# One-core causal attention with a hard-swish layer pair: finer first-layer operations, scores up to four units ahead, three TensorE modes, new keys

## The chip, the cores and the metric

The kernel runs on one core of a Trainium2 chip. The metric is device time in microseconds (us) of one execution, as the median of several. The engines are TensorE (PE: matmuls, and PEld: its weight loads), VectorE (DVE), ScalarE (ACT), GpSimd (POOL) and SyncE (SP, which issues most of the transfers).

## What is computed

The reference is causal attention followed by two dense layers with a hard-swish between them:

```python
scores = (q @ k^T) / 8;  scores[j > i] = -1e9        # 4 batches, 12 heads, 448 positions, 64 wide
attn = softmax(scores);  x = (attn @ v)              # x as 1792 tokens x 768
h = x @ w_in                                         # 768 x 2048
g = h * clip(h + 3, 0, 6) / 6
out = g @ w_out                                      # 2048 x 768
```

Inputs and output are float32; the weights arrive as 64-bit words, from which the kernel makes float32 itself.

## The kernel before

**Units.** Attention is cut into 24 units: a unit is one batch and one pair of heads (`unit`, line 420). A unit loads Q, K and V; multiplies Q and K into scores (line 490, rows in four tiles of 112); reduces each row's bound with VectorE (line 505); takes exponentials with ScalarE, which also sums them (line 512); inverts the sums (lines 522 and 523) and scales the rows (`scaled`, lines 531 and 533); transposes 112x112 blocks on PE (line 553), moves them out of the accumulator memory PSUM, and multiplies them with V (line 566). Its result is one 128-row chunk of x for its batch, split into a high and a low part (`x_split`). Scores use 64 rows of the array for each of the two heads at once, products with V use 64 columns for each head, all else uses the whole array. Units 0 to 5 make their scores from the raw float32; later ones split Q and K first and use three terms.

**Layers.** A product of split operands takes three matmuls (`triple`, lines 640 to 642): high by high, high by low, low by high. Four batches of 448 tokens (g = 0 to 3) go through. `first_layer(g)` for the first two batches makes 16 chunks of the hidden layer, each summed over six chunks of x; each chunk of weights needs words turned into floats by VectorE (lines 603, 605 and 608), a high part from ScalarE (line 361) and a low part (line 373). Batch 0's second layer follows in part in `early_products`; the rest of the work runs through sums and differences of half matrices (`middle`, `last_first`, `last_second`), which the change touches through keys alone.

**What sets the order.** Nothing is issued at run time by choice. `Flow` (line 111) is a planner: every piece of work is an operation with a key, an engine or a choice of engines, a duration and dependencies. `Flow.run` plays the program through and at each moment gives a free engine the ready operation with the lowest key whose buffers are free; the order so found is the order of instructions. PE operations have a mode: `tiled` is true for scores and products with V, false for the rest. The planner counts `SWITCH / 2` for each change and stays in a mode while an operation of that mode has a key no more than `KEEP` above the lowest (lines 229 to 233). A unit's key is its `step` plus `UNIT[at]`; loads come at that key plus `T_LOAD + LOADS[at]`, V's another `T_V` later, scores at `K_SCORES`, transposes at `K_TURN`, the product with V at `K_PRODUCT` after it. Units of batch 0 have the lowest keys.

**Limits.** A unit's scores wait for the product of the unit two earlier, or `DEPTH` earlier in batch 0 (line 498). There are eight PSUM banks; a unit's scores take six (`ps`), the first-layer accumulators at most `MOST["mo"]`. Before the order is played out, `Flow.WARM` small matmuls run (line 1092); between 20 and 36 us the planner may put small filler matmuls (line 1072) into gaps of PE.

Of the kernel before, what the change touches and what calls it, by code (L numbers as in the profile page):

```python
# [19 lines left out]
C = 112  # L20
# [8 lines left out]

T_FIRST = -113
T_PACE = 4
T_EARLY = 8
T_EACH = 11
T_LATE = 74
T_DENSE = 7.25
T_LOAD = -8
T_W = 10
T_WLOAD = 9  # L40
T_XA = 166
T_X = 175
T_LAST = 182
T_PAIR = 10.5
T_SECOND = T_LAST + 8 * T_PAIR
T_SECOND_GROUP = 72
T_MID = 120
T_BACK = 40
T_WORDS = 77
M_LOAD = 20  # L50
E_WORDS = 6.5
K_SCORES = 0
K_TURN = 6.5
K_TURNS = 0.6
K_PRODUCT = 14
K_GATE = 5
KEEP_FULL = 0
KEEP_TILED = 6.5
N_RAW = 6
DEPTH = 3  # L60
A_FIRST = 4
D_FIRST = 0.4
T_V = 11
FINE = 3
W_FROM = 3
W_BEHIND = 4
UNIT = [-80, -17, 5, 2.5, 0.5, -1, -2, -1.5, 5.5, 0.5, -6.5, -3, -3.5, -8, -2.5, -4.5, -1, -1.5, -6, -4.5, -2.5, 1, -4, 3]
LOADS = [-70, -38, -8, 10, 0, -10, 12, -14, -22, -4, -20, -14, 10, 4, -12, 2, -8, -12, -2, -28, -10, -4, 4, -6]
K_KEEP = -4
K_G = 4  # L70
GATE_FROM = 1
WORDS = [1, 8, -6, 4, -3, 7, -5, 0, -4, 3, -6, 0, 6, -2, 7, -4, 2, 4, 2, 3, -2, 2, -8, -4, 8, 3, -7, 5]
T_ISSUE = 0.36
NORM_LAG = 1.5
A_LAG = 0

BUFS = dict(
# [6 lines left out]
    qk="d qk", op="d op", wf="d wf", sf="d sf", x="d x", pt="d pt", pr3="d pr3", pr20="d pr20", xq="d xq", xc="d xc", gt="d gt", gm="d gm", so="d so",  # L84
    ps="b s most ps", tp="b s most", av="b s", mo="b mo", c="b c",
)
MOST = dict(qk=3, op=4, wf=4, sf=6, x=8, pt=6, pr3=4, pr20=5, xq=6, xc=21, gt=12, gm=9, so=3, s=8, most=8, ps=8, mo=2, c=8)

ORDERED = dict(sf=3, wd=0, wh=1, wl=2, xq=3, xc=3, gt=3, gm=3, pr3=4, pr2=5, pr1=6, pr20=9, pt=7, op=8)

# [20 lines left out]
class Flow:  # L111
# [3 lines left out]

    FILL, SPARE_TIME, FILL_FROM, FILL_UNTIL = 0.2, 0.25, 20.0, 36.0
    BEGIN, LATENCY = 0.8, 0.12
    SWITCH = 0.4
    TAIL = dict(PE=.1, D=.085, A=.105, P=.04, SP=0)

    KEEP = KEEP_FULL, KEEP_TILED
    QUEUE, WARM = 8, 4
    DMA_PACKET, DMA_RATE, DMA_LANES, DMA_LATENCY = 0.008, 23e3, 16, 2.1
    COLD = dict(PE=(4.5, 1.6), SP=(7.5, 1.3))
    FIRST_UNTIL, FIRST_DMA = 34.0, 1.18
# [4 lines left out]
        self.filler, self.idle, self.spare = None, 0.0, 1  # L130
        self.ops, self.wrote, self.readers, self.landed = [], {}, {}, []

    def op(self, key, ways, parts, r=(), tiled=False, nbytes=0):

        w = [x for _, _, ws in parts for x in ws]
        bufs = {x[0] for x in list(r) + w if isinstance(x[0], Buf)}
        o = Op((key, len(self.ops)), ways, parts, bufs, nbytes)
        o.tiled = tiled
        for b in bufs:
            b.refs += 1  # L140
        before = {}
        for x in list(r) + w:
            if x in self.wrote:
                a, i = self.wrote[x]
                before[a] = max(before.get(a, 0), i)
        for x in w:
            for a in self.readers.pop(x, ()):
                before[a] = len(a.parts) - 1
        for x in r:
            self.readers.setdefault(x, []).append(o)  # L150
        for i, (_, _, ws) in enumerate(parts):
            for x in ws:
                self.wrote[x] = o, i
        before.pop(o, None)
        for a, i in before.items():
            a.then.append((o, i))
        o.waits = len(before)
        self.ops.append(o)
        return o

    def run(self):

        events, out = [], []
        lists = {e: [] for e in ("PE", "D", "A", "P", "SP")}
        busy = dict.fromkeys(lists, self.BEGIN)
        self.dma, self.mode, self.port, tick = 0.0, False, 0.0, 0
        left = len(self.ops)

        def post(t, what, x):
            nonlocal tick  # L170
            tick += 1
            heappush(events, (t, tick, what, x))

        post(self.BEGIN, "idle", None)
        turns, seen = {k: [] for k in ORDERED.values()}, set()
        for o in self.ops:
            if not o.waits:
                post(0.0, "ready", o)
            for b in o.bufs - seen:
                if b.kind in ORDERED:  # L180
                    turns[ORDERED[b.kind]].append((o.key, o))
            seen |= o.bufs
        for x in turns.values():
            x.sort(key=lambda a: a[0], reverse=True)
        while events:
            now = events[0][0]
            while events and events[0][0] <= now + 1e-9:
                _, _, what, x = heappop(events)
                if what == "ready":
                    for e, (_, lag) in x.ways.items():  # L190
                        if lag:
                            post(now + lag, "way", (e, x))
                        else:
                            insort(lists[e], (x.key, x), key=lambda a: a[0])
                elif what == "way":
                    if x[1].ends is None:
                        insort(lists[x[0]], (x[1].key, x[1]), key=lambda a: a[0])
                elif what == "end":
                    left -= 1
                    for b in sorted(x.bufs, key=lambda b: b.at):  # L200
                        b.refs -= 1
                        if not b.refs:
                            self.slots[b.tag].append(b.slot)
                            for t in b.uses:
                                self.free[t] += 1
            for e, cand in lists.items():
                if busy[e] > now + 1e-9:
                    continue
                cand[:] = [a for a in cand if a[1].ends is None]
                chosen, limit = None, 1e9  # L210
                for _, o in cand:
                    if o.key[0] > limit:
                        break
                    if e in o.port and (self.port > now + 1e-9 or e == "D" and self.turn_of_pool(o, lists["P"], busy, now)):
                        continue
                    need = {}
                    for b in o.bufs:
                        if not b.held:
                            for t in b.uses:
                                need[t] = need.get(t, 0) + 1  # L220
                    for b in o.bufs:
                        if not b.held and b.kind in ORDERED:
                            x = turns[ORDERED[b.kind]]
                            while x and x[-1][1].ends is not None:
                                x.pop()
                            if x[-1][1] is not o:
                                need[b.tag] = len(self.ops)
                    if all(self.free[t] >= n for t, n in need.items()):
                        if e != "PE" or o.tiled == self.mode:
                            chosen = o, need  # L230
                            break
                        if not chosen:
                            chosen, limit = (o, need), o.key[0] + self.KEEP[self.mode]
                if e == "PE":
                    if not chosen:
                        self.spare = min(self.spare, self.free["b"])
                    else:
                        self.fill(now, out)
                if chosen:
                    self.start(chosen[0], e, now, chosen[1], out, busy, post)  # L240
        assert not left, [o.key for o in self.ops if o.ends is None][:5]
        out.sort(key=lambda a: a[:2])
        return out
# [21 lines left out]
    def start(self, o, e, now, need, out, busy, post):  # L265
# [3 lines left out]
            b.held, b.slot = True, self.slots[b.tag].popleft()  # L269
        t, o.ends = now, []  # L270
        if e == "PE" and o.tiled != self.mode:
            t += self.SWITCH / 2
            self.mode = o.tiled
        for d, emit, _ in o.parts:
            out.append((t, len(out), e, emit, o.port))
# [26 lines left out]
def tile_causal_attention_hardswish_moe(ctx: ExitStack, tc: tile.TileContext, q, k, v, w_in, w_out, out):  # L302
    nc = tc.nc
# [38 lines left out]
        if not port:  # L342
            o.port = set()

    def pe(key, parts, r, tiled=False):
        flow.op(key, {"PE": (1, 0)}, [(d, lambda e, g=g: g(), w) for d, g, w in parts], r, tiled)

    def dma(key, packet, o, i, r=(), w=(), queue="SP", rows=128):
# [71 lines left out]
    def unit(b, p):  # L420
        at = NPAIR * b + p
# [67 lines left out]
                    qx, kx = (ap(xs[x])[:, 0], ap(xs[y])[:, 1]) if xs else (qa(0), qa(1))  # L489
                    nc.tensor.matmul(score(e, i), qx[m, c], kx[m, :w], start=n == 0, stop=n == len(terms) - 1)  # L490

        cost, more = (1.667e-3, .06) if raw32 else (1.25e-3, .08)
        for a, two in enumerate(((1, 0), (3, 2)) if at == 0 else ((3, 2), (1, 0))):
            key = t + 2 * a + K_SCORES
            pe(
                key,
                [(cost * C * (i + 1) + more, lambda i=i: products(i), [(ps[e, i][0], i) for e in range(2)] + [("turn",)]) for i in two],
                (halves_[0] if at == a == 0 else reads) + [("unit", at - (2 if b else DEPTH))], True,
            )
            for i in two:  # L500
                w = C * (i + 1)
# [40 lines left out]
        for e in range(2):  # L542
            for js, ph in zip(GROUPS, pairs):
# [8 lines left out]
                    for n, (i, j) in enumerate(blocks):  # L552
                        nc.tensor.transpose(ap(tp)[:C, C * n:C * n + C], row_of(pr, e, i)[:, C * j:C * j + C], ident)  # L553

                pe(key, [(.096 * len(blocks) + .03, turn, [(tp, 0)])], [pk[e, i] for i in sorted({i for i, _ in blocks})])
                move(
                    key + .1, o, lambda ph=ph, e=e, o=o: ap(ph)[:, e, :o], lambda tp=tp, o=o: ap(tp)[:C, :o],
                    [(tp, 0)], [(ph, e)], {"A": 1, "D": (1, .4 if b else D_FIRST)},
# [9 lines left out]
                        start=(j == 0), stop=(j == NC_ - 1),  # L568
                    )

        pe(t + K_PRODUCT, [(10 * C * 1.667e-3, times_v, [(av, 0), (av, 1), ("unit", at)])], deps, True)
        if b < 2:
            x_split(t + 16, b, p, av, S)
        else:
# [71 lines left out]
    def first_layer(g):  # L646
# [5 lines left out]
        for i in range(NF):  # L652
            t = t0 + 3 * i
            wh, wl = weights(g, i, t)
            acc, r = bank("mo"), buf("r", [128, S])
            few = 1 if not g and i < FINE else 2
            for c0 in range(0, NK, few):
                cs = range(c0, c0 + few)

# [429 lines left out]
    b = Buf("b", [128, 512], F32)  # L1089
    b.slot = BANKS["b"] - 1  # L1090
    for _ in range(Flow.WARM):
        nc.tensor.matmul(ap(b)[:C, :C], warm, warm, start=True, stop=True)

    sync = mybir.DependencyInfo(mybir.DependencyClass.Sync, mybir.DependencyReason.DATA)
    older = None
# [46 lines left out]
```

## Time and profile before

| | us |
|---|---|
| median of 3 runs | 583.35 (583.2 to 584.42) |
| the profiled execution, its own time | 583.93 |
| its span, first to last instruction | 582.2 |
| PE busy | 573.8 |
| DVE busy | 486.7 |
| ACT busy | 405.7 |
| POOL busy | 233.4 |

The busy times are those of one profiled execution. PE's matmuls overlap one another and their ends are modelled, so its busy time is no measure of lost time; the starts of its instructions in the timeline are. "Idle before" in a row is the time in which an engine had nothing to do, with what ended it.

### The profile page before, as it was taken

To read this page: it belongs to the slowest core of one execution; us is meant where nothing else is said; L and a number is where in the kernel's file an instruction comes from. 1 tells how busy PE (TensorE), PEld (TensorE's weight loads), DVE (VectorE), ACT (ScalarE), POOL (GpSimd) and SP (SyncE) were. 2 spreads that over 40 slices of the span, in tenths; PEclk is the share of its full clock that TensorE was granted. 3 is DMA by queue.
4 is the path that set the end of the run, shared out by engine and by line. 5 is a ranking of instruction groups with operands and counts; after the bars stand their busy time and mean duration, and the time that the engine had idled before them with its cause. 6 is when DMAs were issued, how large, how long until landed. Compare 5 with 4: busy or idle time off the path is not lost.

```text
span 582.2 us, 10686 instructions
## 1 busy us (share of the span) xinstructions
PE 573.8 (99%) x3496; PEld 502.5 (86%) x3496; DVE 486.7 (84%) x1093; ACT 405.7 (70%) x973; POOL 233.4 (40%) x226
## 2 busy tenths in 40 slices
PE   8999999999999999999999999999999999999997
PEld 5667988988888788888988989899999999999996
DVE  5899999899689787999998668999888799985652
ACT  6997885888757666899988968576555586454530
POOL 2678889874447344776274212034000042100000
PEclk9999999999999999999999999999999999999999
DMA  8958999967579898999832254441211424443411
GB/s 235 334 184 278 315 319 362 395 230 233 179 267 303 258 385 267 329 381 304 301 114 76 94 165 145 160 128 56 82 55 55 128 64 135 133 133 111 138 64 48
DMA packets 61352, 115.59 MB, mean 199 GB/s; under 512 B 6512, under 2 KB 36592, under 8 KB 61296
## 3 DMA queue, kind: packets, MB, share of 16 engines
q1 hardware_dynamic: 60576, 114.34, 59.5%
q10 hardware_dynamic: 720, 0.57, 0.3%
q8 instruction: 27, 0.44, 0.3%
q14 instruction: 29, 0.24, 0.1%
HBM read 83.39 MB, written 31.49 MB: 197 GB/s over the span
## 4 chain that ended last, share of the span: by engine, by line
PE 88%; DMA 5%; DVE 3%; ACT 2%; issue 1%; SPq 0%; DVEq 0%; ACTq 0%
PE b L640 24%; PE b L641 23%; PE b L642 23%; PE b L566 7%; PE b L553 6%; PE b L490 5%; DMA gl<-in_v_dram 2%; DMA wd<-in_w_in_dram 1%; DMA wd<-in_w_out_dram 1%; ACT d L512 1%; DVE b L603 1%; DVE d L608 1%; DVE b L505 1%; DVE b L605 1%; ACT gl L512 0%
## 5 line engine op out<-in xcount | busy, mean ns | idle before, releaser
L640 PE MATMUL b<-d,wh 128*128 128x448 f32 x624 | 231.4, 371 | 0.7 <-ACT d L512 0.7
L641 PE MATMUL b<-d,wh 128*128 128x448 f32 x624 | 226.3, 363 | 0.0
L642 PE MATMUL b<-d,wl 128*128 128x448 f32 x624 | 225.7, 362 | 0.0
L640 PEld LDWEIGHTS b<-d,wh 128*128 128x128 f32 x624 | 117.2, 188 | 10.6 <-ACT d L512 1.2
L642 PEld LDWEIGHTS b<-d,wl 128*128 128x128 f32 x624 | 116.9, 187 | 9.0 <-POOL wl L373 0.4
L641 PEld LDWEIGHTS b<-d,wh 128*128 128x128 f32 x624 | 117.2, 188 | 6.3
L361 ACT CAST wh<-wd 128x768 fp32r<-128x768 f32 x88 | 73.6, 836 | 70.1 <-PE b L641 61.5
L373 DVE TENSOR_TENSOR wl<-wd,wh 128x768 fp32r<-128x768 f32 x74 | 79.7, 1077 | 26.0 <-ACT wh L361 25.0
L505 DVE CUSTOM_DVE_ANT_0 b<-b,mask 112x224 f32<-112x224 f32 (+1 forms) x192 | 80.2, 479 | 19.6 <-PE b L490 17.2
L512 ACT ACTIVATE d<-b,prow 112x448 f32<-112x448 f32 (+2 forms) x144 | 72.2, 517 | 15.5 <-DVE prow L505 13.1
L373 POOL TENSOR_TENSOR d<-d 128x896 fp32r<-128x896 f32 (+3 forms) x28 | 43.2, 1548 | 36.3 <-DVE d L373 23.4
L553 PE MATMUL b<-ident,d 112*112 112x112 f32 x384 | 55.9, 261 | 1.2 <-ACT d L512 0.8
L373 POOL TENSOR_TENSOR wl<-d,wh 128x768 fp32r<-128x768 f32 (+1 forms) x28 | 46.1, 1649 | 23.9 <-ACT wh L361 14.9
L361 ACT COPY d<-b 112x336 f32<-112x336 f32 (+1 forms) x104 | 43.7, 494 | 7.5 <-PE b L553 6.9
L553 PEld LDWEIGHTS b<-ident,d 112*112 112x112 f32 x384 | 42.7, 133 | 5.6 <-POOL gl L533 1.0
L533 POOL TENSOR_SCALAR d<-d,prow 112x112 f32<-112x112 f32 (+2 forms) x59 | 29.4, 509 | 31.7 <-DVE prow L523 25.4
L566 PE MATMUL b<-d,vr 112*64 112x224 f32 (+3 forms) x288 | 37.5, 405 | 0.0
L531 ACT ACTIVATE d<-d,prow 112x336 f32<-112x336 f32 (+2 forms) x66 | 33.8, 548 | 4.2 <-DVE prow L523 4.2
L603 DVE TENSOR_SCALAR b<-wd 128x384 int32<-128x384 int32 (+1 forms) x56 | 32.9, 613 | 3.0 <-DMA wd<-in_w_out_dram 2.5
L490 PE MATMUL b<-d 64*112 64x448 f32 (+3 forms) x432 | 35.0, 305 | 0.0
L490 PEld LDWEIGHTS b<-d 64*112 64x112 f32 x432 | 30.2, 172 | 5.5 <-issue 1.2
L566 PEld LDWEIGHTS b<-d,vr 112*64 112x64 f32 x288 | 19.1, 136 | 18.4 <-issue 10.7
(111 smaller groups left out, 934.3 us busy)
## 6 DMA issues: line engine op xcount, KB each, us to landing
wd<-in_w_in_dram SPq DMA_DIRECT2D x32, 384.0 KB, 6.0
wd<-in_w_out_dram SPq DMA_DIRECT2D x24, 512.0 KB, 6.6
wd<-kept_w SPq DMA_DIRECT2D x32, 384.0 KB, 4.7
wd<-kept_s SPq DMA_DIRECT2D x32, 384.0 KB, 3.0
kept_w<-d SPq DMA_DIRECT2D x16, 384.0 KB, 6.2
kept_w<-d SPq DMA_DIRECT2D x24, 256.0 KB, 5.4
kept_s<-d SPq DMA_DIRECT2D x24, 256.0 KB, 3.8
wd<-kept_w SPq DMA_DIRECT2D x48, 128.0 KB, 2.2
```

The costliest lines, as they stand in the source:

```text
L361: nc.scalar.copy(o(), i()) if scale is None else nc.scalar.mul(o(), i(), scale)
L373: (nc.gpsimd if e == "P" else nc.vector).tensor_tensor(o(), a(), b(), op)
L490: nc.tensor.matmul(score(e, i), qx[m, c], kx[m, :w], start=n == 0, stop=n == len(terms) - 1)
L505: lambda _, e=e, i=i, w=w: nc.vector.tensor_tensor_reduce(score(e, i), score(e, i), mask[:, S - w:], -0.125, 3.0e38, ALU.add, ALU.min, ap( ...
L512: lambda _, e=e, i=i: nc.scalar.activation(row_of(pr, e, i), score(e, i), ACTF.Exp, bias=ap(st)[:, e, i:i + 1], scale=-1.0, accum_out=ap(s ...
L531: nc.scalar.mul(x, x, ap(st)[:, e, 4 + i:5 + i])
L553: nc.tensor.transpose(ap(tp)[:C, C * n:C * n + C], row_of(pr, e, i)[:, C * j:C * j + C], ident)
L566: nc.tensor.matmul(ap(av)[64 * e:64 * e + 64, S - w:S], va()[:, j, e, :], ap(ph)[:, e, o:o + w], start=(j == 0), stop=(j == NC_ - 1),)
L603: nc.vector.tensor_scalar(ti, high, 3, 0x3FFFFFFF, ALU.logical_shift_left, ALU.bitwise_and)
L640: nc.tensor.matmul(ps, ap(wh)[:, a], xh, start=start, stop=False, skip_group_check=more)
L641: nc.tensor.matmul(ps, ap(wh)[:, a], xl, start=False, stop=False, skip_group_check=more)
L642: nc.tensor.matmul(ps, ap(wl)[:, a], xh, start=False, stop=stop, skip_group_check=more)
```

## The change

- `first_layer`: every planned operation holds one group of three products (`few = 1`); before, two groups, except for the first three chunks of batch 0.
- `DEPTH` 3 to 4: in batch 0 a unit's scores wait for the product of the unit four earlier.
- Modes: full (0), scores (1) and product with V (2). A switch between any two counts 0.1 us (before 0.2, and none between scores and product); `KEEP` is 1 in the full mode and 7 in each of the other two.
- Limits: first-layer accumulators 4 (before 2), and small changes to other buffer kinds.
- Warm-up: 11 calls of 56 columns instead of 4 calls of 112; a float32 call makes two instructions.
- Planner's figures for scores, transposes and products with V, keys rounded to five places, and all keys chosen anew.

```diff
-T_FIRST = -113
-T_PACE = 4
+T_FIRST = -71
+T_PACE = 9.5
...
-T_LOAD = -8
+T_LOAD = -32
...
-K_TURN = 6.5
-K_TURNS = 0.6
-K_PRODUCT = 14
-K_GATE = 5
-KEEP_FULL = 0
-KEEP_TILED = 6.5
+K_TURN = 10
+K_TURNS = 0.3
+K_PRODUCT = 13.5
+K_GATE = 6
+KEEP_FULL = 1
+KEEP_TILED = 7
...
-DEPTH = 3
-A_FIRST = 4
-D_FIRST = 0.4
-T_V = 11
+DEPTH = 4
+A_FIRST = 5.6
+D_FIRST = 0
+T_V = 15
...
-UNIT = [-80, -17, 5, 2.5, 0.5, -1, ...
-LOADS = [-70, -38, -8, 10, 0, -10, ...
+UNIT = [-51, -17, 7, 6, -1.5, -3.5, ...
+LOADS = [-10, -52, -20, -14, -12, 8, ...
...
-MOST = dict(qk=3, op=4, wf=4, sf=6, x=8, pt=6, pr3=4, pr20=5, xq=6, xc=21, gt=12, gm=9, so=3, s=8, most=8, ps=8, mo=2, c=8)
+MOST = dict(qk=3, op=4, wf=4, sf=7, x=8, pt=7, pr3=5, pr20=4, xq=6, xc=21, gt=12, gm=8, so=3, s=8, most=8, ps=8, mo=4, c=8)
...
-    SWITCH = 0.4
+    SWITCH = 0.1
...
-    KEEP = KEEP_FULL, KEEP_TILED
-    QUEUE, WARM = 8, 4
+    KEEP = KEEP_FULL, KEEP_TILED, KEEP_TILED
+    QUEUE, WARM = 8, 11
...
-            t += self.SWITCH / 2
+            t += self.SWITCH
...
-        pe(t + K_PRODUCT, [(10 * C * 1.667e-3, times_v, [(av, 0), (av, 1), ("unit", at)])], deps, True)
+        pe(t + K_PRODUCT, [(10 * C * 1.667e-3 + .07, times_v, [(av, 0), (av, 1), ("unit", at)])], deps, 2)
...
-            few = 1 if not g and i < FINE else 2
+            few = 1
...
-        nc.tensor.matmul(ap(b)[:C, :C], warm, warm, start=True, stop=True)
+        nc.tensor.matmul(ap(b)[:C, :C // 2], warm, warm[:, :C // 2], start=True, stop=True)
```

Other constants that change: `T_WLOAD` 9 to 7, `T_XA` 166 to 150, `T_X` 175 to 172, `T_LAST` 182 to 186, `T_SECOND` stays 266, `M_LOAD` 20 to 12, `K_KEEP` -4 to -6, `K_G` 4 to 1, `NORM_LAG` 1.5 to 1, and the list `WORDS`.

## Rows read from the trace of the kernel before

**Rows 1.** The page: PE's busy share, its granted clock by slices, its costliest group.
```profile
PE 573.8 (99%) x3496; PEld 502.5 (86%) x3496; DVE 486.7 (84%) x1093; ACT 405.7 (70%) x973; POOL 233.4 (40%) x226
...
PEclk9999999999999999999999999999999999999999
...
L640 PE MATMUL b<-d,wh 128*128 128x448 f32 x624 | 231.4, 371 | 0.7 <-ACT d L512 0.7
```

**Rows 2.** Waits of PE, whole span: total us, times, longest us.
```profile
PE b L490 <- DMA gh<-in_k_dram: 1.4, 2, 0.8
PE b L553 <- ACT d L512: 1.1, 2, 0.8
```

**Rows 3.** Timeline of PE at 215.79: start us, us, instruction, [idle before].
```profile
215.79 0.47 PE L640 MATMUL b<-d,wh 128*128 128x448 f32 x1 [0.70 <-ACT d L512]
```

**Rows 4.** Busy time by window: us, PE, PEld, DVE, ACT, POOL, clock, DMA.
```profile
260.00:300.00 40.00, 40.00 (x273) 34.59 (x273) 39.08 (x96) 35.66 (x99) 23.53 (x19) 1.00 0.80 257
```

**Rows 5.** Timeline of the start: warm-up, scores of units 0 and 1, VectorE's wait.
```profile
1.08 1.56 PEld L1092 LDWEIGHTS b<-warm 64*112 64x112 f32 x8 [1.08 <-DVE warm L385]
...
3.58 4.08 PE L490 MATMUL b<-gh 64*112 64x224 f32 x16 [0.67 <-DMA gh<-in_k_dram]
...
8.42 5.96 PE L490 MATMUL b<-gh 64*112 64x448 f32 x32 [0.76 <-DMA gh<-in_k_dram]
...
10.27 0.63 DVE L505 CUSTOM_DVE_ANT_0 b<-b,mask 112x448 f32<-112x448 f32 x1 [1.34 <-PE b L490]
```

**Rows 6.** Groups by form, 8.4 to 10 us, then 12.2 to 14.2: busy, mean ns.
```profile
L490 PE MATMUL b<-gh 64*112 64x448 f32 x4 | 1.8, 1010 | 0.8 <-DMA gh<-in_k_dram 0.8
...
L490 PE MATMUL b<-gh 64*112 64x448 f32 x4 | 0.9, 537 | 0.0
```

**Rows 7.** Timeline around unit 3's scores, PE and then DVE.
```profile
18.26 2.11 PE L566 MATMUL b<-d,gl 112*64 112x448 f32 x16
...
22.64 1.57 PE L490 MATMUL b<-gh 64*112 64x448 f32 x8
...
21.10 0.17 DVE L522 TENSOR_SCALAR b<-prow 112x8 f32<-112x8 f32 x1 [1.60 <-ACT d L512]
...
24.20 0.61 DVE L505 CUSTOM_DVE_ANT_0 b<-b,mask 112x448 f32<-112x448 f32 x1
```

**Rows 8.** Timeline of PE around V with scores, and around scores alone.
```profile
98.20 0.36 PE L641 MATMUL b<-d,wh 128*128 128x448 f32 x1
98.40 0.37 PE L642 MATMUL b<-d,wl 128*128 128x448 f32 x1
98.70 2.11 PE L566 MATMUL b<-d,vr 112*64 112x448 f32 x16
100.74 1.89 PE L490 MATMUL b<-d 64*112 64x448 f32 x24
102.56 0.47 PE L640 MATMUL b<-d,wh 128*128 128x448 f32 x1
102.87 0.37 PE L641 MATMUL b<-d,wh 128*128 128x448 f32 x1
...
211.02 0.36 PE L642 MATMUL b<-d,wl 128*128 128x448 f32 x1
...
213.46 0.37 PE L641 MATMUL b<-d,wh 128*128 128x448 f32 x1
```

**Rows 9.** Timeline of PE around seven transposes between products.
```profile
183.79 0.36 PE L642 MATMUL b<-d,wl 128*128 128x448 f32 x1
...
184.88 0.37 PE L641 MATMUL b<-d,wh 128*128 128x448 f32 x1
```

**Rows 10.** Timeline of PE: the first tiled run after 60 us, the last.
```profile
71.98 2.11 PE L490 MATMUL b<-d 64*112 64x448 f32 x24
...
364.13 2.11 PE L566 MATMUL b<-d,vr 112*64 112x448 f32 x16
```

More of the change, by code (lines that the diff above doesn't have):

```diff
@@ L37 @@
 T_DENSE = 7.25
-T_LOAD = -8
+T_LOAD = -32
 T_W = 10
[L40 to L43, printed above, removed]
+T_WLOAD = 7
+T_XA = 150
+T_X = 172
+T_LAST = 186
 T_PAIR = 10.5
-T_SECOND = T_LAST + 8 * T_PAIR
+T_SECOND = 266
 T_SECOND_GROUP = 72
@@ L49 @@
 T_WORDS = 77
-M_LOAD = 20
+M_LOAD = 12
 E_WORDS = 6.5
 K_SCORES = 0
-K_TURN = 6.5
-K_TURNS = 0.6
-K_PRODUCT = 14
-K_GATE = 5
-KEEP_FULL = 0
-KEEP_TILED = 6.5
+K_TURN = 10
[4 more added lines that the diff above has]
+KEEP_TILED = 7
 N_RAW = 6
-DEPTH = 3
-A_FIRST = 4
-D_FIRST = 0.4
-T_V = 11
+DEPTH = 4
+A_FIRST = 5.6
+D_FIRST = 0
+T_V = 15
 FINE = 3
@@ L66 @@
 W_BEHIND = 4
[L67 to L70, printed above, removed]
+UNIT = [-51, -17, 7, 6, -1.5, -3.5, -8, -2.5, 6, -2.5, -6.5, -4.5, -6, -7.5, -4.5, -6, -6.5, -3.5, -8, 0, -3.5, 2, -4.5, -1.5]
+LOADS = [-10, -52, -20, -14, -12, 8, -18, 0, -28, -4, 8, -16, 8, -30, -24, -8, 12, -26, -26, 6, 2, -16, 2, 12]
+K_KEEP = -6
+K_G = 1
 GATE_FROM = 1
-WORDS = [1, 8, -6, 4, -3, 7, -5, 0, -4, 3, -6, 0, 6, -2, 7, -4, 2, 4, 2, 3, -2, 2, -8, -4, 8, 3, -7, 5]
+WORDS = [5, 5, 3, 1, 3, 7, -3, 8, -2, 0, 8, 2, 6, 6, 1, 4, 3, -1, -8, 5, -5, 7, -5, 0, -6, 3, 0, -4]
 T_ISSUE = 0.36
-NORM_LAG = 1.5
+NORM_LAG = 1
 A_LAG = 0
@@ L131, in __init__, with op @@
         self.ops, self.wrote, self.readers, self.landed = [], {}, {}, []
-    def op(self, key, ways, parts, r=(), tiled=False, nbytes=0):
+    def op(self, key, ways, parts, r=(), tiled=0, nbytes=0):
         w = [x for _, _, ws in parts for x in ws]
         bufs = {x[0] for x in list(r) + w if isinstance(x[0], Buf)}
-        o = Op((key, len(self.ops)), ways, parts, bufs, nbytes)
+        o = Op((round(key, 5), len(self.ops)), ways, parts, bufs, nbytes)
         o.tiled = tiled
@@ L165, in run @@
         busy = dict.fromkeys(lists, self.BEGIN)
-        self.dma, self.mode, self.port, tick = 0.0, False, 0.0, 0
+        self.dma, self.mode, self.port, tick = 0.0, 0, 0.0, 0
         left = len(self.ops)
@@ L343, in one, with pe @@
             o.port = set()
-    def pe(key, parts, r, tiled=False):
+    def pe(key, parts, r, tiled=0):
         flow.op(key, {"PE": (1, 0)}, [(d, lambda e, g=g: g(), w) for d, g, w in parts], r, tiled)
@@ L490, in products @@
                     nc.tensor.matmul(score(e, i), qx[m, c], kx[m, :w], start=n == 0, stop=n == len(terms) - 1)
-        cost, more = (1.667e-3, .06) if raw32 else (1.25e-3, .08)
+        cost, more = (1.667e-3, .06) if raw32 else (1.25e-3, .09)
         for a, two in enumerate(((1, 0), (3, 2)) if at == 0 else ((3, 2), (1, 0))):
@@ L497, in unit @@
                 [(cost * C * (i + 1) + more, lambda i=i: products(i), [(ps[e, i][0], i) for e in range(2)] + [("turn",)]) for i in two],
-                (halves_[0] if at == a == 0 else reads) + [("unit", at - (2 if b else DEPTH))], True,
+                (halves_[0] if at == a == 0 else reads) + [("unit", at - (2 if b else DEPTH))], 1,
             )
@@ L553, in turn @@
                         nc.tensor.transpose(ap(tp)[:C, C * n:C * n + C], row_of(pr, e, i)[:, C * j:C * j + C], ident)
-                pe(key, [(.096 * len(blocks) + .03, turn, [(tp, 0)])], [pk[e, i] for i in sorted({i for i, _ in blocks})])
+                pe(key, [(.096 * len(blocks), turn, [(tp, 0)])], [pk[e, i] for i in sorted({i for i, _ in blocks})])
                 move(
```

## The prediction

> **What bounds the kernel now.** I read the page's busy shares first: TensorE (PE) 99% of the span [rows 1]. Since ends of matmuls are modelled, that share alone proves little, so the second view is the waits of PE: its largest entries are 1.4 us for a load and 1.1 us for ScalarE [rows 2]. The reader is to see how little that is, and in the timeline where it lies: after 48 us there is one wait alone, 0.70 us at 215.79 [rows 3]. The third view is PE's starts in the steady part. Products of 448 columns start every 0.20 us (98.20 and 98.40 [rows 8]); line 640 issues 624 of its commonest form [rows 1], and with lines 641 and 642 that alone is 3 x 624 x 0.20 = 374 us of the 582. PE is therefore bound by its own instruction stream from about 54 us on. What a new order can still win there is changes of mode and that one wait. What it can win before 54 us is idle time of the attention start-up, where the softmax engines (VectorE, ScalarE) pace PE. VectorE is also near full later, 39.08 of 40 us between 260 and 300 [rows 4], without making PE wait there; so it has little room if the order gets worse.
>
> **The change, part by part.** Sums are made against the profiled execution: span 582.2 us, own time 583.93 us, that is 1.73 us around the span. The median shown is 583.35, so 0.58 us comes off at the end.
>
> *Start: warm-up of 22 short matmuls instead of 8, and other load keys.* Before, the eight warm-up instructions start at 1.08 us; PE is then idle 0.67 us, works on unit 0's scores from 3.58, idles 0.76 us and takes unit 1's scores at 8.42 when K has landed [rows 5]. Up to there it runs at half rate: the four 64x448 score matmuls of unit 1 take 1.8 us, those of unit 2, after 12.2 us, 0.9 us [rows 6]. By their durations that is the lower and the upper level (1.2 and 2.4 GHz); the page's line of granted clock reads full in every slice [rows 1] and does not show it. The rise came within the unbroken series of 5.96 us that starts at 8.42. Eleven calls of 56 columns are 22 instructions. The eight took 1.56 us by their weight loads, 0.195 each. If one of half the columns takes half, the 22 end at 1.08 + 22 x 0.098 = 3.2 us, before the first data: no delay, and the first gap is all but filled. If the weight load, still of 112 columns, sets the pace, 22 x 0.195 ends at 5.4 us, 1.8 us late. I take the former, since matmuls of full width hide their loads in all rows of the steady part. The load keys put unit 1's Q and K ahead of unit 0's V: now -164 (unit 0), -162.5 (unit 1), V at -149; before, V of unit 0 at -260 stood ahead of unit 1 at -172. On SP's queue V, one issue of 224 KB, no longer stands before them. PE's wait of 0.76 us bounds what that can give. V of unit 0, now behind, is needed at 18.26 us and has room.
> What is this worth? VectorE waits 1.34 us for unit 1's first scores (10.27 us) [rows 5], and the rest of its row follows at its own pace. So of the 1.8 us at stake in PE's rate and the 0.76 us of the landing, the softmax chain can use 1.34 us. Value -1.3 us, bounds -2.5 (0.76 + 1.8) and +1.8.
> On that rate, the Trainium skill (TensorE: Matmul & The Clock Gate, Part 1: The HAM clock gate) says that the array starts at half clock, is released by sustained activity, and that the moment varies between runs. Rows 6 agree on the half rate; no run here shows the moment varying. By that rule this piece would be worth 0 to 1.8 us of PE time and not a fixed amount.
>
> *Scores up to four units ahead.* Unit 3's scores waited for unit 0's product, which starts at 18.26 and takes 2.11 us; they start only at 22.64, and VectorE, idle 1.60 us before 21.10, meanwhile took up weight words and reduces unit 3's scores first at 24.20 [rows 7]. With DEPTH 4 the dependency goes. Next late are banks: a unit's score operation needs four at once, and unit 2's free up as ScalarE finishes its exponentials; the 1.60 us of VectorE is put down to just that. So the scores can come perhaps at 20 us, VectorE has work in most of its 1.60 us. Value -1.2, bounds -1.6 and 0 (if banks hold them until 21.1).
>
> *First layers in operations of three products, four accumulators instead of two.* No instruction is added: the same 192 groups of three (576 products), cut into 192 planned operations instead of 105. The finer cut lets transposes in more often. Such an excursion is nearly free: from the last product before (183.79) to the second after (184.88) is 1.09 us; less two normal spacings 0.69 us for seven transposes [rows 9], 0.10 each, and 0.096 is what the planner's own line counts for a transpose alone. In the start, more accumulators let the products of units 0 to 2 for chunks 2 and 3 stand in where PE waits for ScalarE (1.1 us) [rows 2]. But each chunk also wants VectorE's words first, close to 3 us of them (between VectorE's two rows in rows 7), on an engine that has none to spare. Value -0.5, bounds -1.4 and 0.
>
> *Three modes.* Today scores and products with V count as one mode and the planner keeps to it: after 60 us PE's timeline has 18 runs of scores and products with V that hold 35 groups, the first at 71.98, the last at 364.13 [rows 10], so 17 joins. The price of a broken join: V and scores together, from the product at 98.40 to the second after, 102.87, cost 4.47 - 0.40 = 4.07 us; scores alone, 211.02 to 213.46, 2.44 - 0.40 = 2.04; V alone would be 2.04 (98.70 to 100.74) plus 0.10 on entry and 0.11 on return (102.56 to 102.87 against 0.20), 2.25. Together 4.29, so 0.22 us a join [rows 8]. Bounds: all 17 broken, +3.7; none broken and the 0.7 us of rows 3 gone, -0.7. In the planner the switch now costs 0.1 and the keep of 7 applies to each mode alone, but the scores of a unit become ready when the product two units before ends, so most stay neighbours by key. I take three broken: +0.6.
>
> *Everything else* (keys of later loads, buffer limits, rounded keys, cost figures) I put at 0: PE's queue of products covers a late load, as PE's one wait after 60 us shows. Without that cover a piece costs about what that one did, 0.7 us. The end, from the last product on, is untouched.
>
> Sum: -1.3 - 1.2 - 0.5 + 0.6 = -2.4; 583.93 - 2.4 = 581.5, less 0.58: **580.9 us**.
>
> **Rivals.**
> *A. The start gives much more.* With the clock up before unit 1, no wait for unit 3 and PE's idle time filled, the terms at their far ends are -2.5 - 1.6 - 1.4 = -5.5, and with the 0.7 us -6.2: 577.2. For it: all PE waits but one lie there. Against: VectorE's and ScalarE's work in the start is unchanged.
> *B. Given back.* The start gains 1 to 2 us and VectorE, full at 260 to 300 us, or later keys make PE wait two or three times 0.7 us; or the clock still rises at 12 us and banks still hold unit 3. Then 583.3. Against: VectorE's load is the same, only earlier.
> *C. Slower: broken joins.* Place: every product with V between 72 and 366 us. Price 0.22 us each, at most 17, +3.7. It decides from 14 broken joins at my start gain of 3.0, from 7 if the start gains half. With 17 broken and a start gain of 1.0: 583.35 + 2.7 = 586.0. For it: the change is just that V no longer counts as the mode of scores, and a keep of 1 now also holds PE in full mode. Against: neighbouring keys.
> *D. The warm-up overruns.* Paced by its weight loads it ends at 5.4 us, the first scores are 1.8 us late unit 3 with them, so that of the other gains only the 0.5 us of the first layers stays: 583.35 + 1.8 - 0.5 = 584.7. For it: 0.195 us is also the time of the full-width call, so the two can't be told apart. Against: if so, the clock rises earlier.
>
> **How the numbers follow.** Less than 0.2% (1.2 us) is no change here. Chances: my forecast 0.44 (own range 579.3 to 582.2), A 0.18, B 0.16, C 0.14, D 0.08. Faster is the forecast and A: 0.62. Same is B and a part of D: 0.18. Slower is C and the rest of D: 0.20. The range runs from A, 577.0, to near C, 585.5, and leaves out the far half of each.
>
> **What would show it.** Right: half-rate score matmuls end before unit 1's; VectorE no longer waits 1.3 us before unit 1; unit 3's scores start before 21 us without a filler ahead; PE goes over to unbroken first-layer products some 3 us earlier; tiled runs after 60 us stay near 20. Wrong: unit 1's 64x448 scores still take 1.8 us for four; first scores later than 3.6 us (D); 25 or more tiled runs (C); waits of PE after 60 us of more than 1 us in all (B).

## The result and the profile after

The changed kernel takes 587.64 us in the median (586.94 to 589.81), the kernel before 583.35 us. The ratio is 1.0073, with a 95% interval of 1.0048 to 1.0099. It is slower, where I had forecast 580.9 us. The profiled execution took 587.05 us with a span of 585.3 us, 3.1 us more than the span before; the rest of this part takes these 3.1 us apart.

From the page after: busy time, clock by slices, and the costliest group, as in [rows 1].

```profile
PE 576.0 (98%) x3502; PEld 505.6 (86%) x3502; DVE 486.9 (83%) x1100; ACT 400.2 (68%) x961; POOL 235.3 (40%) x231
...
PEclk9999999999999999999999999999999999999999
...
L640 PE MATMUL b<-d,wh 128*128 128x448 f32 x624 | 231.4, 371 | 0.0
```

TensorE's work is the same (six more warm-up and filler records). What changed is where it waits and how often it changes its mode. The four largest waits of PE after, whole span, to be read beside [rows 2, 3]:

```profile
PE b L553 <- ACT d L512: 2.6, 4, 1.4
PE b L566 <- issue: 1.1, 1, 1.1
PE b L1092 <- DVE warm L385: 1.1, 1, 1.1
PE b L566 <- ACT d L512: 0.9, 1, 0.9
```

The 0.7 us at 215.79 is gone; after 60 us a wait of 1.4 and one of 1.1 us stand in its place. The timeline of the start after, PE, to be read beside [rows 5, 7]:

```profile
1.08 4.17 PE L1092 MATMUL b<-warm 64*112 64x56 f32 x21 [1.08 <-DVE warm L385]
4.86 0.71 PE L490 MATMUL b<-gh 64*112 64x224 f32 x1
5.04 0.39 PE L1092 MATMUL b<-warm 64*112 64x56 f32 x1
5.23 4.27 PE L490 MATMUL b<-gh 64*112 64x224 f32 x16
...
18.44 1.69 PE L490 MATMUL b<-gh 64*112 64x448 f32 x8
20.05 2.11 PE L566 MATMUL b<-d,gl 112*64 112x448 f32 x16
```

The warm-up runs until 5.23 us, and the first scores start at 4.86 instead of 3.58. Unit 3's scores do start ahead of unit 0's product, at 18.44 instead of 22.64. VectorE reduces them at 20.27 instead of 24.20, and its two waits of 1.34 and 1.60 us are gone; its longest wait between 8 and 26 us is now 0.30 us. But it takes up unit 0's first scores 1.6 us later, and has waited that much longer by then. VectorE's timeline, two lines after and one before:

```profile
6.81 0.40 DVE L505 CUSTOM_DVE_ANT_0 b<-b,mask 112x224 f32<-112x224 f32 x1 [5.04 <-PE b L490]
...
20.27 0.63 DVE L505 CUSTOM_DVE_ANT_0 b<-b,mask 112x448 f32<-112x448 f32 x1
```

```profile
5.20 0.40 DVE L505 CUSTOM_DVE_ANT_0 b<-b,mask 112x224 f32<-112x224 f32 x1 [3.44 <-PE b L490]
```

TensorE's clock did rise earlier in this execution: unit 1's four 64x448 score matmuls take 1.2 us instead of 1.8 [rows 6] (groups by form, 8.8 to 12 us).

```profile
L490 PE MATMUL b<-gh 64*112 64x448 f32 x4 | 1.2, 578 | 0.0
```

I then went through PE's starts block by block (a block is a run of one kind) and took from each block its work at the steady spacing: 0.2004 us for a product of 448 columns, 0.096 for a transpose, and the streaming time of the columns for scores and V. What is left over is lost time:

| stretch | before | after |
|---|---|---|
| start, to the end of unit 5's product | 51.62 us, 15.9 lost | 52.58 us, 15.9 lost (1.0 us more scores done by then) |
| later: full-mode products | 10.9 lost in 62 blocks | 12.2 in 71 |
| later: transposes | -1.4 | 0.8 |
| later: scores and V | 11.2 | 10.8 |
| later, all | 20.6 lost | 23.7 lost |

The start gave nothing, and the 3.1 us come after it: 1.3 at full-mode products, where there are more changes of mode, 2.2 at transposes, where two new waits stand against the old one of 0.7, less 0.4 at scores and V. The groups of scores or products with V after 60 us are 35 as before, now in 27 tiled runs instead of 18, so 8 joins instead of 17. A broken join looks like this (PE, after): V at 71.96 goes back to products, and the scores follow at 77.80, where [rows 8] had them together.

```profile
71.67 0.36 PE L642 MATMUL b<-d,wl 128*128 128x448 f32 x1
71.96 2.11 PE L566 MATMUL b<-d,vr 112*64 112x448 f32 x16
74.00 0.47 PE L640 MATMUL b<-d,wh 128*128 128x448 f32 x1
74.31 0.36 PE L641 MATMUL b<-d,wh 128*128 128x448 f32 x1
...
77.51 0.36 PE L642 MATMUL b<-d,wl 128*128 128x448 f32 x1
77.80 1.89 PE L490 MATMUL b<-d 64*112 64x448 f32 x24
79.63 0.47 PE L640 MATMUL b<-d,wh 128*128 128x448 f32 x1
79.94 0.37 PE L641 MATMUL b<-d,wh 128*128 128x448 f32 x1
```

Read as the prediction reads [rows 8], from the last product before to the second after, V costs 2.64 - 0.40 = 2.24 us here (71.67 to 74.31) and the scores 2.43 - 0.40 = 2.03 us (77.51 to 79.94). Together that is 4.27 us where the joined pair cost 4.07: 0.20 us a join, 1.8 us for the 9 that are gone. The table's rows for products, scores and V show only 0.9 us more, because short stalls of 0.2 to 0.3 us that the kernel before has at scores and products (at 72.0, 240.0 and 242.1 us) are gone.

The first new wait, in the timeline after (SP, ScalarE, PE):

```profile
181.65 0.64 SPq L352 DMA_DIRECT2D kept_s<-d  x1
...
186.18 0.54 ACT L512 ACTIVATE d<-b,prow 112x336 f32<-112x336 f32 x1 [2.27 <-DMA kept_s<-d]
...
186.87 0.31 PE L553 MATMUL b<-ident,pr 112*112 112x112 f32 x1 [1.41 <-ACT d L512]
```

An exponential is to be written into a `d` buffer from which a sum of weights is still being written out; the last such transfer before it was issued at 181.65, ScalarE stands until 186.18, and PE waits for what ScalarE makes. The page's median from issue to landing of these write-outs is 5.0 us, 3.8 before. The second, at 232.64, is V waiting 1.11 us for a copy of transposed blocks, which VectorE takes up only after two sums of the middle stage (the profile names no releaser there; I read the copy from the times):

```profile
231.50 0.63 DVE L373 TENSOR_TENSOR gl<-gh,gl 128x448 f32<-128x448 f32 x1
232.04 1.45 DVE L364 COPY d<-b 112x336 f32<-112x336 f32 x3
...
232.64 1.25 PE L566 MATMUL b<-d,vr 112*64 112x448 f32 x6 [1.11 <-issue]
```

### The profile page after: what moved, and what is told of

Its sections match the earlier page's. It is cut to its first block, busy times and chain, and to the rows that moved or that the text cites. A ratio compares the mean times of both kernels' runs of the same rounds, so it can differ in the third digit from the quotient of the medians.

```text
span 585.3 us, 10698 instructions
## 1 busy us (share of the span) xinstructions
PE 576.0 (98%) x3502; PEld 505.6 (86%) x3502; DVE 486.9 (83%) x1100; ACT 400.2 (68%) x961; POOL 235.3 (40%) x231
## 4 chain that ended last, share of the span: by engine, by line
PE 93%; ACT 2%; DVE 2%; DMA 2%; issue 0%; DVEq 0%; ACTq 0%
PE b L640 24%; PE b L642 24%; PE b L641 23%; PE b L566 8%; PE b L553 7%; PE b L490 6%; DMA d<-kept_w 1%; ACT d L512 1%; DVE b L505 1%; PE b L1092 1%; ACT gl L512 1%; DVE d L364 0%; DMA vr<-in_v_dram 0%; ACT d L361 0%; DVE prow L505 0%
## 5 line engine op out<-in xcount | busy, mean ns | idle before, releaser
L373 DVE TENSOR_TENSOR wl<-wd,wh 128x768 fp32r<-128x768 f32 x72 | 73.8, 1025 | 24.4 <-ACT wh L361 23.4
L533 POOL TENSOR_SCALAR d<-d,prow 112x336 f32<-112x336 f32 (+2 forms) x65 | 35.4, 555 | 47.3 <-DVE d L373 27.3
L361 ACT COPY d<-b 112x336 f32<-112x336 f32 (+1 forms) x97 | 41.4, 483 | 8.8 <-PE b L553 6.6
L373 POOL TENSOR_TENSOR d<-d 128x896 fp32r<-128x896 f32 (+2 forms) x20 | 33.8, 1693 | 20.8 <-ACT d L361 19.2
L373 DVE TENSOR_TENSOR d<-d 128x512 f32<-128x512 f32 (+3 forms) x46 | 36.1, 793 | 4.0 <-DMA d<-kept_x 1.2
L373 POOL TENSOR_TENSOR wl<-wd,wh 128x768 fp32r<-128x768 f32 x16 | 29.5, 1848 | 23.1 <-PE b L490 15.1
L566 PEld LDWEIGHTS b<-d,vr 112*64 112x64 f32 x288 | 19.3, 136 | 19.1 <-issue 10.8
L373 POOL TENSOR_TENSOR wd<-wd 128x384 f32<-128x384 f32 x9 | 9.0, 1018 | 65.7 <-DVE wl L373 47.4
```

Source lines behind the costliest of these rows:

```text
L361: nc.scalar.copy(o(), i()) if scale is None else nc.scalar.mul(o(), i(), scale)
L373: (nc.gpsimd if e == "P" else nc.vector).tensor_tensor(o(), a(), b(), op)
L533: (nc.gpsimd if w == "P" else nc.vector).tensor_scalar(x, x, ap(st)[:, e, 4 + i:5 + i], 1.0, ALU.mult, ALU.mult)
L566: nc.tensor.matmul(ap(av)[64 * e:64 * e + 64, S - w:S], va()[:, j, e, :], ap(ph)[:, e, o:o + w], start=(j == 0), stop=(j == NC_ - 1),)
```

## The experiments

My theory after this reading has three losses: the warm-up that overruns, two waits behind in-order engines, and broken joins. The rival is that the new order is worse everywhere, so that taking one loss away only uncovers another. Kernels that keep an order keep it on all five engines. All ratios are against the kernel before.

**The dependency by itself.** With only `DEPTH` at 4, the plan of the kernel before comes out the same, instruction for instruction, on every engine. So it was not run. So in the old order the dependency alone did not hold unit 3's scores. In the new one they run ahead of unit 0's product (18.44 and 20.05), which `DEPTH` 3 forbids: the move took the new keys and the new depth together.

**The old warm-up in the changed kernel, the new one in the kernel before.** Both keep their orders.

```diff
-    QUEUE, WARM = 8, 11
+    QUEUE, WARM = 8, 4
...
-        nc.tensor.matmul(ap(b)[:C, :C // 2], warm, warm[:, :C // 2], start=True, stop=True)
+        nc.tensor.matmul(ap(b)[:C, :C], warm, warm, start=True, stop=True)
```

> The changed kernel with the old warm-up (4 calls of 112 columns), all else and the whole order as changed. Warm-up theory: in the changed kernel the 22 short instructions start every 0.187 us, so unit 0's first scores start at 4.86 us although their data are there at 3.6; here they start at 3.6 and the two heads' matmuls run in step again, so 1.3 to 2.2 us come back: 585.4 to 586.3. Rival, the softmax engines pace the start: nothing comes back, 587.6.

> The kernel before with the new warm-up (11 calls of 56 columns) and nothing else. Warm-up theory: first scores at 4.9 us instead of 3.6, 1.3 to 2.2 us slower than before: 584.7 to 585.5. Rival: the longer work of TensorE brings its clock up before unit 1's scores and pays for that: 582 to 583.4.

The first took 586.64 us, ratio 1.0060 (1.0037 to 1.0083), span 583.9; the second 585.24 us, ratio 1.0032 (1.0019 to 1.0046). With the old warm-up, PE of the changed kernel (timeline of its start) gets to the scores of units 0 and 1 early:

```profile
1.08 1.83 PE L1092 MATMUL b<-warm 64*112 64x112 f32 x8 [1.08 <-DVE warm L385]
3.56 3.62 PE L490 MATMUL b<-gh 64*112 64x224 f32 x16 [0.64 <-DMA gh<-in_k_dram]
7.73 1.54 PE L490 MATMUL b<-gh 64*112 64x448 f32 x7 [0.56 <-DMA gh<-in_k_dram]
```

The span is 1.4 us shorter, and unit 5's product ends at 51.05 instead of 52.58. The change of the median, 1.0 us, is under what I expected and its interval overlaps that of the changed kernel; its two longest executions (588.27 and 588.41 us) have a mean granted clock of 0.997, the other four of 0.999 or more. The swap in the kernel before shows the loss clearly: 0.32%, 1.9 us. Not all of it lies in the start: in the profiled execution PE is 0.6 us behind at the end of unit 5's product (52.21 instead of 51.62), and 0.9 of the 1.8 us between the spans is a wait for VectorE at 253.89 us that the kernel before has not. By the medians, then, the new warm-up costs 1 to 2 us in either order. The load keys are hard to read: unit 1's scores start at 7.73 instead of 8.42, but with the old load keys that start lies between 7.80 and 8.71 in six profiled kernels, so the gain is anything from 0.1 to 1.0 us.

**Which part of the warm-up costs.** First 6 calls of 56 columns in the kernel before, then 11 calls over all 128 rows.

```diff
-    QUEUE, WARM = 8, 4
+    QUEUE, WARM = 8, 6
...
-        nc.tensor.matmul(ap(b)[:C, :C], warm, warm, start=True, stop=True)
+        nc.tensor.matmul(ap(b)[:C, :C // 2], warm, warm[:, :C // 2], start=True, stop=True)
```

> The kernel before with a warm-up of 6 calls of 56 columns (12 instructions, at 0.187 us they end at 3.4 us, before the first data). Step theory: in the changed kernel the clock does rise some 3 us earlier, but the gain is lost because the warm-up overran and put the two heads' score matmuls out of step; here neither happens, so unit 1's four 64x448 matmuls take 0.9 us instead of 1.8 and 1 to 2 us are won: 581.5 to 582.5. Rival, the clock rises at 12 us whatever is done ahead of 3.6 us: no change, 583.3.

> The kernel before with the new warm-up (11 calls of 56 columns), but over all 128 rows of the array, so that it blocks both heads' halves alike. Step theory: the first scores are as late as with the new warm-up (4.9 us) but in step; unit 2's scores take 2.0 us again instead of 2.9, and the loss of the new warm-up (1.9 us by medians) falls to about 0.5 or turns into a gain: 582.5 to 584. Rival, lateness alone counts: 585.2 as with the new warm-up.

```diff
-    QUEUE, WARM = 8, 4
+    QUEUE, WARM = 8, 11
...
-    warm = const.tile([64, C], F32, tag="warm", name="warm")
+    warm = const.tile([128, C], F32, tag="warm", name="warm")
```

Six calls: 583.66 us, ratio 0.9998 (0.9986 to 1.0010). Over all rows: 585.49 us, ratio 1.0037 (1.0025 to 1.0049). The theory of heads out of step fell: in step, the loss stayed, which leaves the lateness of the first scores (5.38 us there). With six calls nothing was won. Their profiled execution shows an earlier clock that did not last. Busy time by window of that kernel, first, and then its transposes of unit 0 in PE's timeline:

```profile
0.00:10.00 10.00, 8.32 (x38) 5.61 (x39) 4.86 (x22) 5.08 (x17) 0.75 (x6) 1.00 0.81 228
10.00:20.00 10.00, 8.91 (x55) 6.68 (x54) 8.83 (x42) 9.08 (x32) 5.73 (x12) 0.83 1.06 280
...
14.38 0.28 PE L553 MATMUL b<-ident,d 112*112 112x112 f32 x1 [0.80 <-ACT d L512]
...
15.39 1.23 PE L553 MATMUL b<-ident,d 112*112 112x112 f32 x6
```

Unit 1's scores did go to full rate, at about 8.9 us, and unit 0's transposes started 0.8 us earlier (14.38 against 15.19). After the wait of 0.80 us for ScalarE the clock fell again, the mean of 10 to 20 us being 0.83, and six transposes took 1.23 us, which at full rate take 0.74.

That an earlier clock is worth nothing does not follow. The kernel with extra matmuls ahead of V (below) is the kernel before up to 60 us, old warm-up and all. In its profiled execution the same 32 score matmuls of units 1 and 2 take 5.13 us instead of 5.96 [rows 5], the clock holds through a wait of 0.81 us, and the first scores of the second batch start at 51.12 instead of 51.62, although K landed 0.3 us later:

```profile
8.71 5.13 PE L503 MATMUL b<-gh 64*112 64x448 f32 x32 [1.07 <-DMA gh<-in_k_dram]
14.66 0.28 PE L566 MATMUL b<-ident,d 112*112 112x112 f32 x1 [0.81 <-ACT d L525]
...
51.12 1.90 PE L503 MATMUL b<-d 64*112 64x448 f32 x24
```

In two more kernels with the old warm-up and the old keys (one extra matmul between V and scores; `few = 1`) unit 1's scores also reach the full rate before 9 us, and the second batch's scores start at 50.67 and 50.97. So the moment at which the clock rises differs between executions of the same start, and a rise that comes early and stays goes with 0.5 to 1.0 us less here. The execution of the kernel before that [rows 5, 6] show is the late one.

**The wait filled.** Six calls, and small matmuls in that wait.

```diff
-                def turn(e=e, blocks=blocks, tp=tp):
+                def turn(e=e, blocks=blocks, tp=tp, more=(8, 3)[c - 1] if at == 0 and c < 3 else 0):
+                    for _ in range(more):
+                        nc.tensor.matmul(ap(tp)[:C, :C], identr, identr, start=True, stop=True)
```

> The kernel before with 6 warm-up calls of 56 columns and, ahead of unit 0's first two groups of transposes, 8 and 3 small full-mode matmuls in the time in which TensorE waits for ScalarE. With 6 calls alone the clock rose at 8.9 us but fell again after that wait, and the transposes of units 0 and 1 ran at half rate (granted clock 0.83 from 10 to 20 us). Clock theory: with the wait filled the clock stays up, the transposes keep full rate and the 0.8 us by which they start earlier is kept: 582.5 to 583.0 where before is 583.5. Rival, the softmax engines pace the start anyway: no change, 583.5.

585.00 us, ratio 1.0033 (1.0021 to 1.0046): not faster, even slower. In the profiled execution, which was its shortest (583.81), the clock stayed at 1.00 from 10 to 20 us, and still the first scores of the second batch start no earlier than before (51.62):

```profile
51.73 1.44 PE L490 MATMUL b<-d 64*112 64x448 f32 x14
```

But the run tests less than I meant. The added matmuls themselves take the time that was to be won: they start at 14.54, and unit 0's first transpose only at 15.37, where six calls alone had 14.38 and the kernel before 15.19.

```profile
14.54 1.00 PE L553 MATMUL b<-identr 112*112 112x112 f32 x8 [0.72 <-ACT d L512]
15.37 0.28 PE L555 MATMUL b<-ident,d 112*112 112x112 f32 x1
```

So neither the clock theory nor the rival is shown by it. Why the other executions were longer stays open.

**A join broken by one matmul.** One extra matmul of 112 columns in the kernel before, between V and scores, or ahead of V; the core of it:

```diff
+        if one_more[0]:
+            nc.tensor.matmul(o, identr, identr, start=True, stop=True)
...
+            extra(score(0, i)[:, :C])       # between: first thing of the 12 marked score operations
...
+            extra(ap(av)[:C, :C])           # ahead: first thing of the 12 marked products with V
```

> The kernel before with one extra full-mode matmul (112x112) between a product with V and the scores right behind it, at the 12 places after 60 us where these two adjoin. Theory of broken joins: each costs its own 0.1 us and 0.2 for leaving and entering the mode: 12 x 0.32 = 3.8 us more than before, 587.2. Rival, a change between the two tiled modes costs as much as one by way of the full mode: 12 x 0.1 = 1.2 us, 584.6.

> The same 12 extra matmuls, but ahead of the product with V, where TensorE is in the full mode or comes from scores anyhow. Both theories: their own time alone, 12 x 0.1 = 1.2 us more than before, 584.6, and up to 0.3 for each place where scores stood right ahead of that product.

Between: 585.83 us, ratio 1.0038 (1.0020 to 1.0056). Ahead: 584.42 us, ratio 1.0015 (1.0003 to 1.0026). Ahead costs 1.1 us, 0.09 each, its own time. Between costs 1.4 us more by the medians, 0.12 a join, midway between the two theories. One place in PE's timeline of the first kernel (its lines are shifted):

```profile
97.79 2.11 PE L580 MATMUL b<-d,vr 112*64 112x448 f32 x16
99.83 0.31 PE L333 MATMUL b<-identr 112*112 112x112 f32 x1
100.06 0.46 PE L503 MATMUL b<-d 64*112 64x448 f32 x2
```

Scores start 2.27 us after V, where [rows 8] have 2.04: 0.23 us, of which 0.10 is the matmul itself. So a join that this small matmul breaks costs 0.12 to 0.13 us beyond the matmul. The changed kernel breaks its joins with products of 448 columns, and there the rows above give 0.20.

**The wait for the buffer.** The changed kernel in its own order, with write-outs of weight sums of 32 of 256 columns, and loads of the same size from the plain weights (the sums are left out of the later products).

```diff
-                    t - T_W + 3, 1024, lambda o=o, m=m, r=r: kept_s[...].rearrange("c p w -> p c w"),
+                    t - T_W + 3, 1024, lambda o=o, m=m, r=r: kept_s[...].rearrange("c p w -> p c w")[:, :, :32],
...
-                lambda j=j, hh=hh, cc=cc: kept_s[j, hh, cc], ...
+                lambda j=j, hh=hh, cc=cc: kept[NF + 2 + hh:NF + 2 + hh + 9:4, :, 256 * cc:256 * cc + 256].rearrange("m p w -> p m w"), ...
```

> The changed kernel in its own order, with the write-outs of weight sums cut to 32 of 256 columns; the loads that follow take the plain weights from the other store, at the same size, so the weight sums are left out of the later products. Theory of the buffer wait: ScalarE's wait of 2.27 us at 186.18 us for such a write-out to release its buffer goes, and with it TensorE's 1.41 us: 1.4 less than the changed kernel, 586.2 where that was 587.6, and no wait of TensorE near 185 us. Rival, the next operand is late anyway: TensorE waits there for something else, 587.6.

585.64 us, ratio 1.0035 (1.0023 to 1.0047); span 584.1 against 585.3. In its timeline ScalarE's exponential follows the one before without a wait:

```profile
183.78 0.54 ACT L512 ACTIVATE d<-b,prow 112x336 f32<-112x336 f32 x1
184.20 0.21 ACT L512 ACTIVATION_READ_ACCUMULATOR d<-b,prow 112x1 f32 x1
```

PE's wait of 1.41 us is gone too. The intervals of this kernel and of the changed one do not overlap. The lighter transfers did nothing elsewhere: PE's instructions start within 0.03 us of those of the changed kernel up to that wait, 1.8 us earlier right behind it and 1.3 us earlier from 240 us on.

**Both losses taken away.** The old warm-up and the short write-outs together.

> The changed kernel in its own order with both the old warm-up and the short write-outs of weight sums (weight sums left out of the later products). If the two losses add, 1.5 and 1.2 us by the spans, it is 2.7 us below the changed kernel: span 582.6, time about 584.3, within 1 us of before. What then stays is the broken joins (about 1.2 us) and the wait of 1.1 us at 232 us, against about 1.5 us that the new start wins. Rival, the order is bad throughout and other waits take their place: 586 or more.

583.97 us, ratio 1.0016 (1.0003 to 1.0030), span 581.8. PE's waits after 60 us in that kernel:

```profile
PE b L566 <- PE b L553: 0.5, 1, 0.5
```

The two losses add. The span lies 3.5 us under that of the changed kernel, more than the 2.7 expected, since the wait at 232 us shrank as well. What is left, 0.16%, I take to be broken joins against the gain of the new start; no run parts the two. Up to unit 5's product the kernels with the new order and the old warm-up lose 14.3 and 14.8 us, the four with the start of before 14.9 to 15.9. The 15.9 is the execution in which the clock rose last.

**Planned anew: V counted as scores again, and the finer operations alone.**

```diff
-        pe(t + K_PRODUCT, [(10 * C * 1.667e-3 + .07, times_v, [(av, 0), (av, 1), ("unit", at)])], deps, 2)
+        pe(t + K_PRODUCT, [(10 * C * 1.667e-3 + .07, times_v, [(av, 0), (av, 1), ("unit", at)])], deps, 1)
```

> The changed kernel with products with V counted as the mode of scores again; the plan is made anew, with 17 joins after the start instead of 8. Theory of broken joins: 9 joins at 0.12 to 0.16 us come back, 1.1 to 1.4 us: 586.2 to 586.5, if the new plan opens no other waits; the trace should show 60 us and later with less time in changes of mode. Rival, the loss lies in waits that any new plan meets: waits of TensorE after 60 us of 2 us or more remain or grow, 587 to 590.

```diff
-            few = 1 if not g and i < FINE else 2
+            few = 1
```

> The kernel before with first layers in operations of three products and nothing else; the plan is made anew and holds 62 blocks of transposes between products after the start instead of 51, at the same 17 joins. Theory: the finer cut costs next to nothing by itself, 11 x 0.02 us: 583.5 to 584, unless the new plan opens waits. Rival, each excursion costs what a broken join does, 11 x 0.14 = 1.5 us: 585.

The first, a change of the changed kernel: 588.34 us, ratio 1.0088 (1.0073 to 1.0103). The second, of the kernel before: 588.31 us, ratio 1.0089 (1.0076 to 1.0102). Waits of PE after 60 us, in one and the other:

```profile
PE b L553 <- ACT d L512: 2.1, 1, 2.1
PE b L640 <- ACT d L512: 0.2, 1, 0.2
```

```profile
PE b L553 <- ACT d L512: 0.7, 1, 0.7
PE b L566 <- ACT r L361: 0.6, 1, 0.6
PE b L553 <- ACT d L531: 0.2, 1, 0.2
```

In the first the joins are back, but PE has a new wait of 2.1 us for ScalarE and the start is later, so the rival was right about this kernel. Behind that wait, which ends at 188.46, the granted clock fell as well. Busy time by window:

```profile
190.00:193.00 3.00, 3.00 (x14) 2.75 (x13) 1.43 (x8) 2.25 (x10) 2.42 (x2) 0.50 0.68 251
```

In the second, scores and V fall into 41 groups instead of 36, and lost time after the start is 24.9 us instead of 20.6. Both kernels tell little of the part that they were to isolate, since the plan around it changed; the price of the finer cut by itself stays open. They do show what a new plan does here: of three that were run in full (the changed kernel and these two), each came out 0.7 to 0.9% slower. No version beat the kernel before.

## Why the prediction was wrong

- **The start (-1.3 us): wrong sign, and the step that failed is the pace of the warm-up.** I took half the columns for half the time. The instructions start every 0.187 us as before, so my rival D was right about the overrun: the warm-up ended at 5.2 us (I had 5.4). The reason that I gave against it, that matmuls hide their loads, came from products of 448 columns, and these have 56. VectorE's 1.34 us did go, but its wait for unit 0's first scores grew by 1.6, so nothing came of it at 52 us. The clock did not need the longer warm-up either: with the old one it rose before 9 us in three of four profiled kernels that start as before, and I had read the fourth. By the runs this term was +1 to +2.
- **Unit 3 (-1.2 us) and the first layers (-0.5 us).** The rows came as foretold: scores at 18.44, VectorE without waits. Together with the load keys the new order's start is worth 0.1 to 1.6 us, where I had 3.0 with the warm-up's share; part of that spread is the moment at which the clock rose. The dependency by itself did nothing.
- **Broken joins (+0.6 us).** The price was right, 0.20 us by the rows of the changed kernel where I had 0.22. The step that failed is the count, that most groups stay neighbours by their keys: 9 joins broke instead of 3, +1.8. Rival C, with 14 or more as its point of decision, did not decide alone, but its sign, 25 or more tiled runs, came (27).
- **"Everything else" at 0: the dearest mistake beside the start.** I let PE's queue of products cover a late transfer. It does not when an in-order engine stands for that transfer and PE's next operand comes from it. The write-out that kept a buffer cost 1.4 us of PE in one place (1.2 us of the span, 0.38% by the ratios), and VectorE's order another 1.1. My sign for it, more than 1 us of waits after 60 us, came with 2.5. My rival B had named waits of this kind, though as something that only gives back a gain. Which of the new limits and keys put that exponential and that write-out on one buffer was not tried.

In sum, by the profiled executions: in the start +1.5 for the warm-up and -1.5 for the new order; behind it +1.8 for joins, +2.5 for the two new waits and -0.7 for the old one, together 3.6 where the spans differ by 3.1. The short stalls of the kernel before that are gone are about the rest. The two figures of the start move by up to a microsecond from execution to execution; the -1.5 is measured against the start whose clock rose late.

## What to carry to other kernels

When an order is planned anew, price the whole plan and not only the parts that were meant to change. In a kernel that is full to a few microseconds, the waits it opens on in-order engines, for buffers that a transfer still holds, are as large as what is to be won, and each plan opens its own. And a stand-in matmul that is cut to fewer columns gets shorter only until its weight load sets the pace: cut the calls, and let it end before the first data. And before a gain is put down to an earlier clock, see in more than one execution of the old kernel when its clock rises.

## What the runs showed of the hardware

- Warm-up instructions with weights of 64x112 start 0.187 us apart whether 112 or 56 columns follow, at the lower of TensorE's two levels of clock. I take the weight load to set that pace, since it is what stayed the same.
- A run of products between V and scores costs 0.20 us beyond its own work (4.27 against 4.07 us), one matmul of 112 columns there 0.12 to 0.13 us beyond its own 0.10.
- The level is visible in durations before the clock column shows it: in the kernel before, matmuls ran at the lower level until about 12 us, and the column read 1.00 throughout. With the same warm-up and order the rise came before 8.8 us in another execution. With six calls the clock was up by 8.9 us, and behind a wait of 0.80 us the granted clock averaged 0.83 from 10 to 20 us; behind a wait of 2.1 us in a full stretch it was 0.50 from 190 to 193 us. A wait of 0.81 us in the start did not always bring it down. The Trainium skill (TensorE: Matmul & The Clock Gate, Part 1: The HAM clock gate) has the clock depend on recent activity; the runs agree, and they add that an early rise can be lost again in the same start.
